# A second buffer for VectorE's first product, and four-column tiles moved by two transfers each, in a fused FFT filter and gated feed-forward kernel

## The chip, the cores and the metric

The kernel runs on one core of a Trainium2 chip. Its time is device time in microseconds, from launch to end, for one execution. The core has these engines: PE (TensorE, matrix products), DVE (VectorE), ACT (ScalarE), POOL (GpSimd) and SP (SyncE, which here issues every transfer). Sixteen DMA engines move the data between HBM and the on-chip memory SBUF. PE writes its products to a third memory, PSUM, from which VectorE and ScalarE read.

## The reference

The input x has 8 batches of 3136 rows and 256 columns. The reference filters each batch along its rows in the frequency domain and puts the result through a gated feed-forward layer:

```
X = rfft(x, axis=1)
y = irfft(X * (filt_r + 1j * filt_i), n=3136, axis=1)
h = relu(y @ w_in)                       # 256 -> 1024
c[s] = cw[0]*h[s-1] + cw[1]*h[s] + cw[2]*h[s+1]    # per column of h, zero at both ends
out = (h * sigmoid(c)) @ w_out           # 1024 -> 256
```

Everything is float32 for the filter. The weights of the second part come as float64 and are converted on the chip (`to_f32`, L154 to L174).

## The kernel before, in words

**Two parts.** The first part computes the filtered y as matrix products: 3136 = 28 x 112, so a transform of length 3136 is done as transforms of 112 and 28 with tables. It has four product stages, named `first` (L323), `second` (L330), `third` (L354) and `last_stage` (L210). Between `second` and `third`, `filt` (L341) multiplies with the filter. Between `first` and `second` and between `third` and `last_stage` the data is turned round through HBM, in `a_dram` and `b_dram`. The second part (from L420) is the feed-forward layer for all eight batches, in 448 passes; while it runs on batch b - 1, the last stage of batch b is done in small pieces between its passes.

**Groups.** In the first part the unit of work is a group: four of the 28 columns of a batch, 112 partitions of 4 x 256 float32 values. So each partition's row is 4 KB, and a tile is 448 KB. A batch has NQ = 7 groups, all batches 56.

**One turn of the loop** (L371 on, index i, with m = i - 9) does this, in the order of the program. On SP: load x of group i + 3 (`load`, L300), load a of group m + 1, load a part of the filter tables t1, t2 and of the table i1 in the turns 4 to 10 (`load_tables`, L255). On VectorE and POOL: `filt` of group m - 1. On PE: `first` of group i. ScalarE copies its product to a tile sa, which SP stores to `a_dram` (`store`, L310). On PE: `third` of group m - 2; ScalarE copies it to sb, which SP stores to `b_dram`. On PE: `second` of group m. Then, from turn 11, two steps of the weight conversion (`convert_weights`, L282), which run on VectorE, POOL and ScalarE. From turn 60 on, the last stage of batch 0 is done in seven steps of four columns (`last_load`, `last_stage`, `last_out`, L411 to L417).

**filt** makes three VectorE products from PSUM: `u = pp * t1` (L347), then two halves of v (L348 and L349), and POOL adds them, `z = u + v` (L351). u has one buffer. v has two fixed ones, `turned[0]` and `turned[1]`, chosen by `q % 2`, where q is the group's number in its batch. z and pp have two buffers each.

**Buffers and transfers.** x has four buffers, a three, sa and sb two each. A tile of the filter tables is 64 partitions of 4 KB. Each of these tiles is moved by one transfer. On the side of HBM, rows of x, a, b and the tables are contiguous for 4 KB, and those of the store to `a_dram` for 1 KB. Loads for the last stage (br, L197) are rows of 1 KB; batch 0 uses tiles of four columns with two buffers, the other batches tiles of two columns with four.

**Order.** All transfers go through SP's queue in the order of the program; a transfer that has to wait holds those behind it. The order of PE, VectorE, ScalarE and POOL is also that of the program (`manual_schedule`); semaphores between them are set by the tile framework, which also makes a new use of a buffer wait for the last reader of the old one.

Of the kernel before, what the change touches and what calls it, by code (L numbers as in the profile page):

```python
# [9 lines left out]
F32 = mybir.dt.float32  # L10
# [9 lines left out]
G = 28  # L20
D = 256
# [103 lines left out]
def tile_fft_filter_gated_ffn(  # L125
# [16 lines left out]
    nc = tc.nc  # L142
# [39 lines left out]
    a_dram = [dram.tile([N2, 112, D], F32, name=f"a_dram{b}") for b in range(B)]  # L182
    b_dram = [dram.tile([N2, 112, D], F32, name=f"b_dram{b}") for b in range(B)]
# [11 lines left out]
    lasts = {}  # L195

    def last_load(b, c, n=2):  # L197
        br = lp.tile([112, n, D], F32, name=f"br{n}", bufs=4 if n == 2 else 2)
        nc.sync.dma_start(out=br, in_=b_dram[b][c:c + n].rearrange("n p d -> p n d"))
        lasts[b, c] = br  # L200

# [32 lines left out]
    with (  # L234
# [12 lines left out]
        t1_sb = fc.tile([120, G, D], F32, name="t1_sb")  # L247
        t2_sb = fc.tile([120, G, D], F32, name="t2_sb")
# [6 lines left out]
        def load_tables(c):  # L255

            sl = slice(4 * c, 4 * c + 4)
            nc.sync.dma_start(out=t1_sb[0:64, sl], in_=fr[:, sl])
            nc.sync.dma_start(out=t2_sb[56:120, sl], in_=fi[:, sl])
            nc.sync.dma_start(out=i1_sb[:, sl], in_=i1[:, sl])  # L260

        def copy_filter(c):
# [37 lines left out]
        def load(kind, b, q):  # L300
            if kind == "x":
                r = xp.tile([112, 4, D], F32, name="x", bufs=4)
                v = x[b].rearrange("(p n) d -> p n d", n=N2)
            else:
                r = fp.tile([112, 4, D], F32, name="a", bufs=3)
                v = a_dram[b].rearrange("n (r g) d -> (n r) g d", g=G)
            nc.sync.dma_start(out=r, in_=v[:, 4 * q:4 * q + 4])
            rows[kind, b, q] = r

        def store(kind, b, q, ps):  # L310
            st = (xp if kind == "sa" else fp).tile([112, 4, D], F32, name=kind, bufs=2)
            nc.scalar.activation(st, ps, AF.Copy)  # L312
            sl = slice(4 * q, 4 * q + 4)
            if kind == "sa":
                v = a_dram[b][sl].rearrange("n p d -> p n d")
            else:
                v = b_dram[b].rearrange("n (r g) d -> (n r) g d", g=G)[:, sl]
            nc.sync.dma_start(out=v, in_=st)

        def bank_pair():  # L320
            return fps.tile([128, 1024], F32, name="ps")
# [19 lines left out]
        def filt(b, q):  # L341


            pp, v = psums.pop((b, q)), turned[q % 2]
            sl = slice(4 * q, 4 * q + 4)
            u = fp.tile([120, 4, D], F32, name="u", bufs=1)
            nc.vector.tensor_mul(u, pp, t1_sb[:, sl])  # L347
            nc.vector.tensor_mul(v[64:120], pp[0:56], t2_sb[0:56, sl])  # L348
            nc.vector.scalar_tensor_tensor(out=v[0:56], in0=pp[64:120], scalar=-1.0, in1=t2_sb[64:120, sl], op0=ALU.mult, op1=ALU.mult)  # L349
            z = fp.tile([120, 4, D], F32, name="z")  # L350
            nc.gpsimd.tensor_tensor(out=z, in0=u, in1=v, op=ALU.add)  # L351
            parts[b, q] = z
# [11 lines left out]
        for c in range(4):  # L364
            nc.sync.dma_start(out=s1_sb[:, 4 * c:4 * c + 4], in_=s1[:, 4 * c:4 * c + 4])
            load("x", 0, c)
# [3 lines left out]
        with tc.manual_schedule(engines=COMPUTE):  # L370
            for i in range(NI):  # L371
                m = i - SKEW
                if i == done:
# [4 lines left out]
                    lp = ctx.enter_context(tc.tile_pool(name="lp", bufs=2, side="right", reuse_waits="tile"))  # L378
                if i < 3:
                    nc.sync.dma_start(out=s1_sb[:, 4 * i + 16:4 * i + 20], in_=s1[:, 4 * i + 16:4 * i + 20])  # L380
                if (bp := at(i + 3)) and i:
                    load("x", *bp)
                if bp := at(m + 1):
                    load("a", *bp)
# [4 lines left out]
                if 4 <= i < 11:  # L389
                    load_tables(i - 4)  # L390
                if bp := at(m - 1):
                    filt(*bp)
                pf = first(*bp) if (bp := at(i)) else None
                if pf is not None:
                    store("sa", *at(i), pf)
                pt = third(*bp) if (bp := at(m - 2)) else None
                if pt is not None:
                    store("sb", *at(m - 2), pt)
# [12 lines left out]
                c = 4 * (i - done - 2)  # L411
# [4 lines left out]
                if 0 <= c < N2:  # L416
                    last_load(0, c, 4)  # L417
# [87 lines left out]
    with tc.manual_schedule(engines=COMPUTE):  # L505
        for m in range(NH + PLAG):
            if m + 4 in pieces:
                last_load(*pieces[m + 4])
            if a := at(m):
                inner(*a)  # L510
            if m in pieces:
                last_stage(*pieces[m], ps_h.tile([128, 512], F32, name="ps_h"))
            if a := at(m - PLAG):
                project(*a)
            if a := at(m - 1):
                relu(*a)
                conv(*a)
            if a := at(m - 2):
                gate(*a)
            if a := at(m - 3):  # L520
                split_g(*a)
            if m in pieces:
                last_out(*pieces[m])
            if a := at(m - PLAG):
                evacuate(*a)
# [44 lines left out]
```

## Time and profile before

| what | value |
|---|---|
| time, median of 3 runs | 1641.97 us (1640.53 to 1642.74) |
| profiled execution, its own time | 1637.69 us |
| its span, first to last instruction | 1635.6 us |
| PE busy | 1514.3 us, 93% |
| VectorE busy | 1301.1 us, 80% |
| ScalarE busy | 1171.9 us, 72% |
| POOL busy | 684.2 us, 42% |
| bytes moved | 166.74 MB in 105757 packets |
| granted TensorE clock, mean | 0.983 |

The profile is of one execution. Times in it are in microseconds from the span's start. L347 is line 347 of the kernel. A row of a timeline has the start, the length, the engine, the line, the operation, the tile written and the tiles read, the shapes, and in brackets the idle time before it with what ended it. "SPq" marks SP's issue of a transfer: its length is the issue, not the move. The DMA share is the time of the packets in flight, divided by sixteen engines and the length of the stretch; it can pass 1.00, because packets of one engine overlap a little. A shorter span of an engine that sits idle costs nothing, so what counts is the stage and what ends its waits.

### The profile page before, as it was taken

To read this page: it belongs to the slowest core of one execution; us is meant where nothing else is said; L and a number is where in the kernel's file an instruction comes from. 1 tells how busy PE (TensorE), PEld (TensorE's weight loads), DVE (VectorE), ACT (ScalarE), POOL (GpSimd) and SP (SyncE) were. 2 spreads that over 40 slices of the span, in tenths; PEclk is the share of its full clock that TensorE was granted. 3 is DMA by queue.
4 is the path that set the end of the run, shared out by engine and by line. 5 is a ranking of instruction groups with operands and counts; after the bars stand their busy time and mean duration, and the time that the engine had idled before them with its cause. 6 is when DMAs were issued, how large, how long until landed. Compare 5 with 4: busy or idle time off the path is not lost.

```text
span 1635.6 us, 25256 instructions
## 1 busy us (share of the span) xinstructions
PE 1514.3 (93%) x9424; PEld 1349.6 (83%) x9424; DVE 1301.1 (80%) x1790; ACT 1171.9 (72%) x2043; POOL 684.2 (42%) x568
## 2 busy tenths in 40 slices
PE   5587888887699999999999999999999999999999
PEld 4255555554589999999999999999999999999998
DVE  0388788855688888888888888888888888888887
ACT  2443333331488888888888888888888888888887
POOL 0144544443234444444444444444444444444444
PEclk8699999998999999999999999999999999999999
DMA  9999999986401101111111111111111111100001
GB/s 279 287 310 288 287 289 298 281 252 194 123 23 51 47 29 46 50 48 46 46 47 40 40 46 46 47 36 38 46 35 46 51 47 51 46 23 23 23 24 46
DMA packets 105757, 166.74 MB, mean 102 GB/s; under 512 B 6986, under 2 KB 83875, under 8 KB 105635
## 3 DMA queue, kind: packets, MB, share of 16 engines
q1 hardware_dynamic: 105635, 165.12, 33.7%
q8 instruction: 75, 1.23, 0.3%
q14 instruction: 47, 0.39, 0.1%
HBM read 88.03 MB, written 77.07 MB: 101 GB/s over the span
## 4 chain that ended last, share of the span: by engine, by line
PE 71%; DVE 1%; ACT 1%; issue 0%
PE ps_h L178 11%; PE ps_h L179 11%; PE ps_h L177 11%; PE po L476 11%; PE po L478 11%; PE po L477 11%; PE ps_h L219 5%; ACT y L146 1%; DVE y L149 1%; DVE t L451 0%; PE ps L219 0%; DVE t L450 0%; DVE t L456 0%; ACT sb L312 0%; ACT t L445 0%
## 5 line engine op out<-in xcount | busy, mean ns | idle before, releaser
L152 POOL TENSOR_TENSOR g<-t,g 128x448 fp32r<-128x448 f32 x448 | 517.2, 1155 | 677.9 <-ACT g L146 273.8
L476 PE MATMUL po<-wo,g 128*128 128x256 f32 x1568 | 441.5, 282 | 0.0
L478 PE MATMUL po<-wo,g 128*128 128x256 f32 x1568 | 433.7, 277 | 0.0
L477 PE MATMUL po<-wo,g 128*128 128x256 f32 x1568 | 433.4, 276 | 0.0
L450 DVE SCALAR_TENSOR_TENSOR t<-ps_h,cw,t 128x448 f32<-128x448 f32 x448 | 305.9, 683 | 82.1 <-ACT t L445 71.4
L178 PE MATMUL ps_h<-y,wi 128*128 128x450 f32 x896 | 330.4, 369 | 5.2 <-DVE y L149 5.2
L177 PE MATMUL ps_h<-y,wi 128*128 128x450 f32 x896 | 328.5, 367 | 3.6 <-ACT y L146 1.9
L179 PE MATMUL ps_h<-y,wi 128*128 128x450 f32 x896 | 328.7, 367 | 0.0
L451 DVE SCALAR_TENSOR_TENSOR t<-ps_h,cw,t 128x448 f32<-128x448 f32 x448 | 306.5, 684 | 16.0
L445 ACT ACTIVATE t<-ps_h,cw 128x448 f32<-128x448 f32 x448 | 285.2, 637 | 41.8 <-ACT ps_h L443 0.8
L476 PEld LDWEIGHTS po<-wo,g 128*128 128x128 f32 x1568 | 294.7, 188 | 7.0
L477 PEld LDWEIGHTS po<-wo,g 128*128 128x128 f32 x1568 | 294.3, 188 | 5.7
L478 PEld LDWEIGHTS po<-wo,g 128*128 128x128 f32 x1568 | 294.4, 188 | 0.0
L456 DVE TENSOR_TENSOR t<-ps_h,t 128x448 f32<-128x448 f32 x448 | 275.4, 615 | 0.1
L443 ACT ACTIVATE ps_h<-ps_h 128x450 f32<-128x450 f32 x448 | 251.5, 561 | 32.6 <-PE ps_h L179 28.0
L455 ACT ACTIVATE t<-t 128x448 f32<-128x448 f32 x448 | 254.9, 569 | 12.0 <-DVE t L451 10.8
L146 ACT ACTIVATE g<-t 128x448 fp32r<-128x448 f32 x448 | 254.4, 568 | 0.2 <-DVE t L456 0.2
L351 POOL TENSOR_TENSOR z<-u,v 120x1024 f32<-120x1024 f32 x56 | 142.7, 2548 | 249.7 <-DVE v L349 187.5
L178 PEld LDWEIGHTS ps_h<-y,wi 128*128 128x128 f32 x896 | 168.3, 188 | 14.3 <-DVE y L149 7.5
L177 PEld LDWEIGHTS ps_h<-y,wi 128*128 128x128 f32 x896 | 170.0, 190 | 11.9 <-ACT y L146 2.9
L179 PEld LDWEIGHTS ps_h<-y,wi 128*128 128x128 f32 x896 | 168.3, 188 | 13.9
L358 PE MATMUL ps<-z,i_sb 120*112 120x256 f32 x448 | 115.2, 402 | 68.1 <-POOL z L351 62.5
(51 smaller groups left out, 1411.3 us busy)
## 6 DMA issues: line engine op xcount, KB each, us to landing
x<-in_x SPq DMA_DIRECT2D x56, 448.0 KB, 6.1
a_dram<-sa SPq DMA_DIRECT2D x56, 448.0 KB, 5.3
a<-a_dram SPq DMA_DIRECT2D x56, 448.0 KB, 6.5
b_dram<-sb SPq DMA_DIRECT2D x56, 448.0 KB, 3.3
out<-ot SPq DMA_DIRECT2D x27, 896.0 KB, 4.1
br<-b_dram SPq DMA_DIRECT2D x98, 224.0 KB, 2.6
br<-b_dram SPq DMA_DIRECT2D x7, 448.0 KB, 4.7
raw<-in_w_in SPq DMA_DIRECT2D x8, 256.0 KB, 4.5
```

The lines of the kernel that those rows point to most:

```text
L146: nc.scalar.activation(dst, src, AF.Copy)
L152: nc.gpsimd.tensor_tensor(out=dst, in0=src, in1=hi.bitcast(F32), op=ALU.subtract)
L177: nc.tensor.matmul(ps, lhsT=wh, rhs=rh, start=start, stop=False, **kw)
L178: nc.tensor.matmul(ps, lhsT=wh, rhs=rl, start=False, stop=False, **kw)
L179: nc.tensor.matmul(ps, lhsT=wl, rhs=rh, start=False, stop=stop, **kw)
L445: nc.scalar.activation(t, h[:, 1:SUB + 1], AF.Copy, scale=cw[:, 1, f:f + 1])
L450: nc.vector.scalar_tensor_tensor(out=t, in0=h[:, 0:SUB], scalar=cw[:, 0, f:f + 1], in1=t, op0=ALU.mult, op1=ALU.add)
L451: nc.vector.scalar_tensor_tensor(out=t, in0=h[:, 2:SUB + 2], scalar=cw[:, 2, f:f + 1], in1=t, op0=ALU.mult, op1=ALU.add)
L456: nc.vector.tensor_mul(t, h[:, 1:SUB + 1], t)
L476: nc.tensor.matmul(o, lhsT=gh[:, sl], rhs=wo[0][:, f], start=first, stop=False, skip_group_check=True)
L477: nc.tensor.matmul(o, lhsT=gh[:, sl], rhs=wo[1][:, f], start=False, stop=False, skip_group_check=True)
L478: nc.tensor.matmul(o, lhsT=gl[:, sl], rhs=wo[0][:, f], start=False, stop=last, skip_group_check=True)
```

## The change

u gets the pool's usual two buffers. The transfers of x, a, sa, sb and of the filter tables t1 and t2 are each split into two, of two columns (2 KB a partition) each; for the store to `a_dram` the rows in HBM stay at 1 KB. The tile itself, and what waits for it, is as before: a product that reads a tile waits for both its halves. i1, the transform tables and the weights are moved as before. The tiles br of both sizes become one set of three buffers of four columns, of which a load of two columns uses the first half.

```diff
     def last_load(b, c, n=2):
-        br = lp.tile([112, n, D], F32, name=f"br{n}", bufs=4 if n == 2 else 2)
+        br = lp.tile([112, 4, D], F32, name="br", bufs=3)[:, 0:n]
...
             sl = slice(4 * c, 4 * c + 4)
-            nc.sync.dma_start(out=t1_sb[0:64, sl], in_=fr[:, sl])
-            nc.sync.dma_start(out=t2_sb[56:120, sl], in_=fi[:, sl])
+            for e in (4 * c, 4 * c + 2):
+                nc.sync.dma_start(out=t1_sb[0:64, e:e + 2], in_=fr[:, e:e + 2])
+                nc.sync.dma_start(out=t2_sb[56:120, e:e + 2], in_=fi[:, e:e + 2])
...
-            nc.sync.dma_start(out=r, in_=v[:, 4 * q:4 * q + 4])
+            for e in (0, 2):
+                nc.sync.dma_start(out=r[:, e:e + 2], in_=v[:, 4 * q + e:4 * q + e + 2])
             rows[kind, b, q] = r
...
-            sl = slice(4 * q, 4 * q + 4)
-            if kind == "sa":
-                v = a_dram[b][sl].rearrange("n p d -> p n d")
-            else:
-                v = b_dram[b].rearrange("n (r g) d -> (n r) g d", g=G)[:, sl]
-            nc.sync.dma_start(out=v, in_=st)
+            for e in (0, 2):
+                sl = slice(4 * q + e, 4 * q + e + 2)
+                if kind == "sa":
+                    v = a_dram[b][sl].rearrange("n p d -> p n d")
+                else:
+                    v = b_dram[b].rearrange("n (r g) d -> (n r) g d", g=G)[:, sl]
+                nc.sync.dma_start(out=v, in_=st[:, e:e + 2])
...
-            u = fp.tile([120, 4, D], F32, name="u", bufs=1)
+            u = fp.tile([120, 4, D], F32, name="u")
             nc.vector.tensor_mul(u, pp, t1_sb[:, sl])
```

## The prediction

> **What bounds the kernel now.** I read the page's head for the span, then the windows of busy time, to find the stage that the edit reaches.
>
> ```profile
> span 1635.6 us, 25256 instructions
> ```
>
> ```profile
> 20.00:69.78 49.78, 24.28 (x58) 14.00 (x59) 3.67 (x4) 15.61 (x15) 2.54 (x2) 0.62 1.05 283
> 69.78:97.16 27.38, 22.93 (x88) 14.91 (x86) 24.61 (x20) 15.56 (x15) 10.92 (x5) 1.00 1.02 322
> 69.78:331.51 261.73, 212.88 (x798) 138.64 (x796) 220.14 (x174) 91.63 (x99) 120.97 (x61) 1.00 0.96 292
> 331.51:400.92 69.41, 54.23 (x178) 33.44 (x179) 40.36 (x34) 17.00 (x18) 28.33 (x14) 0.93 0.74 219
> 440.00:1635.60 1195.60, 1181.15 (x8203) 1132.74 (x8201) 1010.43 (x1555) 1028.14 (x1895) 518.19 (x476) 1.00 0.13 41
> ```
>
> The columns of the second fence are the stretch, its length, then busy time and instructions of PE, PEld, DVE, ACT and POOL, the granted clock, the DMA share and GB/s. From 440 us on PE is busy 1181 of 1196 us and DMA 0.13: the edit's transfers and product aren't there. Everything it touches, but for the loads into br, lies in the first 440 us. I chose the ends of the middle stretches at starts of VectorE's first product u, which the view of one tile gives:
>
> ```profile
> L347 DVE TENSOR_TENSOR u<-pp,t_sb x40: 1223/1225/1227, 69.8 to 331.5; 120x1024 f32<-120x1024 f32 x40
> L347 DVE TENSOR_TENSOR u<-pp,t_sb x12: 1224/1225/1226, 331.5 to 400.9; 120x1024 f32<-120x1024 f32 x12
> ```
>
> So a turn of the loop (one group of four columns) takes 261.73/39 = 6.71 us, then 69.41/11 = 6.31 us. What sets it shows in the timeline.
>
> ```profile
> 183.99 1.23 DVE L347 TENSOR_TENSOR u<-pp,t_sb 120x1024 f32<-120x1024 f32 x1
> 185.22 1.22 DVE L348 TENSOR_TENSOR v<-pp,t_sb 56x1024 f32<-56x1024 f32 x1
> 186.46 1.23 DVE L349 SCALAR_TENSOR_TENSOR v<-pp,t_sb 56x1024 f32<-56x1024 f32 x1
> 187.71 0.69 DVE L168 SCALAR_TENSOR_TENSOR ws<-em 128x512 f32<-128x512 int32 x1
> 187.85 2.75 POOL L351 TENSOR_TENSOR z<-u,v 120x1024 f32<-120x1024 f32 x1 [4.18 <-DVE v L349]
> 188.44 2.45 DVE L170 TENSOR_SCALAR em<-ws 128x512 int32<-128x512 int32 x1
> 190.92 1.23 DVE L347 TENSOR_TENSOR u<-pp,t_sb 120x1024 f32<-120x1024 f32 x1
> ...
> 201.46 2.35 POOL L351 TENSOR_TENSOR z<-u,v 120x1024 f32<-120x1024 f32 x1 [2.69 <-PE pp L335]
> 203.84 1.22 DVE L347 TENSOR_TENSOR u<-pp,t_sb 120x1024 f32<-120x1024 f32 x1 [2.55 <-POOL z L351]
> ```
>
> With one u buffer the next u can't start before POOL has read the last one: u, v, v, z, u in a ring. At 203.84 u starts 0.03 us after z ended. In the turn from 183.99 to 190.92 the wait is covered: the weight conversion (L168, L170) fills VectorE until 190.89. Conversion steps come in a cycle of five turns, two of these heavy. VectorE's unavoidable work is 220.14/39 = 5.64 us a turn, PE's 212.88/39 = 5.46. The ring costs the difference to 6.71. But the DMA share in the same stretch is 0.96. So removing the ring exposes the DMA engines almost at once, and the forecast turns on what they can do.
>
> **The change, part by part.** Removed: the wait of u for the last z. Left of the ring are v's two fixed buffers, picked by q % 2. With seven groups in a batch, q = 6 and the next q = 0 share one, so once in seven turns v still waits for z: v, v, z is 1.22 + 1.23 + 2.75 and some 0.3 of releases, 5.5 us, under the forecast turn. That costs nothing here.
>
> Term A, 69.78 to 331.51 us. With the ring gone a turn has three bounds. VectorE has 5.64 us of work in the mean. The two heavy turns of five stay at 6.94 us if nothing smooths them. A third turn holds the conversion step L162:
>
> ```profile
> L162 DVE TENSOR_SCALAR em<-raw 128x512 int32<-128x512 int32 x7 | 15.9, 2265 | 0.0
> ```
>
> That is 3.7 us of products, 2.27, and an estimated 0.4 for the short step ahead of it, 6.4 us; the two light turns fall to PE's 5.5. The five sum to 31.3, so 6.26 a turn. PE: 5.46. The ring z, third, second, product over two turns is below. DMA: a turn moves 292 GB/s x 6.71 us = 1.96 MB at share 0.96. If the price per byte stays and the share rises to 1.00, 1.02 or 1.05 (the last was held from 20 to 69.78 us), a turn is 6.44, 6.32 or 6.13 us; at the 322 GB/s of the first 27 us of this stretch it is 6.09. I take 6.25: among the DMA figures, and the unsmoothed VectorE's figure. Bounds 6.1 and 6.5. That is 39 x (6.71 - 6.25) = 17.9 us less, bounds 24 and 8.
>
> Does a 2 KB row have the price of a 4 KB one? No view tells the 2 KB packets apart, so I bound it by stretches with other mixes.
>
> ```profile
> q1 hardware_dynamic: 46272, 45.42, 13.0%
> ...
> q1 hardware_dynamic: 31453, 67.55, 95.1%
> ...
> DMA packets 803, 2.14 MB, mean 267 GB/s; under 512 B 94, under 2 KB 426, under 8 KB 803
> q1 hardware_dynamic: 803, 2.14, 101.9%
> ```
>
> These are packets, MB and share of 16 engines. The first is 460 to 1600 us, where all is rows of 1 KB: 0.130 x 16 x 1140 us / 45.42 MB = 52 ns per KB. The second is 97.16 to 331.51 us, mostly rows of 4 KB by bytes: 0.951 x 16 x 234.35 / 67.55 = 53 ns. The third is 3 to 11 us, rows of 4 KB and 1.75 KB in one direction: 61 ns. Rows of 1 KB and of 4 KB cost the same here; what moves the price is the direction or the crowding. 2 KB lies between them, so I price the split at nothing per byte, with 3% either way (0.2 us a turn), inside the bounds above. The Trainium skill speaks against this edit: its page Perfetto Trace Analysis, section DMA Optimizations, calls batching small rows, from 2 KB to 4 KB or 8 KB, a dramatic gain in throughput. By that rule the split would raise the turn; the 52 and 53 ns don't bear it out, and how far it could go is the first rival.
>
> The issues double. SyncE's queue in one turn:
>
> ```profile
> 179.90 0.30 SPq L318 DMA_DIRECT2D b_dram<-sb  x1
> 180.30 0.48 SPq L307 DMA_DIRECT2D x<-in_x  x1
> 180.83 0.77 SPq L307 DMA_DIRECT2D a<-a_dram  x1
> 183.35 0.32 SPq L318 DMA_DIRECT2D a_dram<-sa  x1
> ```
>
> Four issues take 1.87 us; eight take up to 3.7 of 6.25, so the queue keeps up. It is in order: a half that waits holds everything behind it, the store after a load too. A second limit shows in its waits and landings:
>
> ```profile
> SPq L260 <- DMA x<-in_x: 3.9, 4, 1.4
> ...
> x<-in_x SPq DMA_DIRECT2D x39, 448.0 KB, 5.9
> a<-a_dram SPq DMA_DIRECT2D x39, 448.0 KB, 6.6
> ```
>
> A load of i1 (L260) waits for a landing of x, with which it shares no data. In those turns x, two table parts, i1 and sa are issued, so that x lies eight issues back: a landing counter seems to come round every eighth transfer. Whole transfers take two turns to come round; halves take one. So each half must land within one turn. The slowest, a, lands after 6.6 us as a whole; less bytes stand ahead of a half (0.23 MB less at 292 GB/s is 0.8 us), 5.8 us, under 6.25. I price it at nothing and keep 6.6 us a turn as a rival.
>
> Term B, 331.51 to 400.92 us, eleven turns. The loads of x end here and DMA falls to 0.74. For the first five turns first() still runs, and PE's 5.46 us is the bound. After that the ring over two turns counts:
>
> ```profile
> 381.47 1.23 DVE L347 TENSOR_TENSOR u<-pp,t_sb 120x1024 f32<-120x1024 f32 x1 [2.54 <-POOL z L351]
> 385.35 2.34 POOL L351 TENSOR_TENSOR z<-u,v 120x1024 f32<-120x1024 f32 x1 [3.92 <-PE pp L335]
> 387.74 1.98 PE L358 MATMUL ps<-z,i_sb 120*112 120x256 f32 x8 [2.56 <-POOL z L351]
> 389.56 1.88 PE L335 MATMUL pp<-a,s_sb 112*120 112x512 f32 x4
> ```
>
> From u to the end of second() behind third() is 391.44 - 381.47 = 9.97 us; that second() feeds the product two turns on, so 5.0 us a turn, 5.1 with releases. 5 x 5.46 + 6 x 5.1 = 57.9 instead of 69.4: 11.5 us less, bounds 13 and 6 (PE's clock, 0.93 here, may fall further).
>
> Behind 400.92 another chain holds:
>
> ```profile
> 427.56 1.95 PE L358 MATMUL ps<-z,i_sb 120*112 120x256 f32 x8 [1.33 <-DVE y L149]
> ```
>
> third() waits for the last stage's output on VectorE, not for z, and I give these turns nothing.
>
> Term C, the start. Up to 69.78 us DMA is the bound (share 1.05), with the price per byte unchanged. The first x is complete one issue later, about 0.4 us, and a few more issues stand ahead of the first store. I take 1.5 us more, bounds 3 less (halves free the window earlier) and 5 more.
>
> Term D, br. Three shared buffers stand in place of four small and two large.
>
> ```profile
> SPq L199 <- PE ps_h L219: 682.3, 94, 27.2
> br<-b_dram SPq DMA_DIRECT2D x98, 224.0 KB, 2.6
> ```
>
> SyncE stands at L199 until a buffer comes free; then the load takes 2.6 us. With three it waits for the stage three pieces back, not four; out's stores are queued behind it, and they wait for later work anyhow. Pieces lie some three to four passes apart, a pass 1195.6/448 = 2.7 us, so the load still lands two pieces, over 16 us, ahead. Price nothing; without that cover 2.6 us for each late load.
>
> Sum: 17.9 + 11.5 - 1.5 = 27.9 us less. The profiled execution took 1637.69 us (span 1635.6), so 1609.8; the median of the three runs is 4.3 above it, so 1614.1.
>
> **The rivals.** *Rows of 2 KB cost more (slower).* With the ring gone, DMA is the bound from 0 to 331.51 us, so a rise f of its price costs f x (70 + 39 x 6.25) = f x 314 us against 27.9 gained: it decides at f = 9%. At 15% the time is 1642 + 19 = 1661 us. Against it stand 52 and 53 ns; for it, that no view separates the packets of 2 KB. 6%. It is the way in which the rule of the Trainium skill's page Perfetto Trace Analysis, section DMA Optimizations, would act here.
>
> *The DMA engines are full already, or the window of eight holds the turn at a's 6.6 us.* Then A gives 39 x 0.11 = 4, B 9 and C -1: 1630 us. For it: share 0.96, and 283 GB/s at 1.05 early on. Against it: 322 GB/s from 69.78 to 97.16 us, with more than one direction in flight, and halves land sooner. 18%.
>
> *DMA has room.* Its share counts packets in flight and may fall when they overlap better; then VectorE's 5.64 is the turn, A gives 42, and the time is 1642 - 52 = 1590 us; that asks 1.96 MB in 5.64 us, 348 GB/s, above the 322 of the best stretch here. 11%.
>
> *The wait stays* by v's pair or by another release in the ring: 1642 us. The code shows one pair per parity, so 2%.
>
> **How the numbers follow.** The forecast has 63%, its own range 1604 to 1631 by the bounds of the terms. The range 1601 to 1634 takes in the full-DMA rival and leaves out the first and third. A measurement of this kernel can tell about 0.2%, 3.3 us, from no change. Faster by more: the forecast, the third rival and most of the second, 0.88. Within: the last one and the second's edge, 0.05. Slower: the first rival and mishaps of the window, 0.07.
>
> **What would show it.** Right: u no longer waits for z; a turn near 6.25 up to about 312 us, DMA share 1.0 or above, PE or VectorE waiting for a; then turns near 5.1 to 5.5; the stretch behind unchanged in length, begun some 28 us sooner. Wrong: DMA below 0.95 with turns under 5.9; or more than 58 ns per KB; or SyncE waiting long at its loads for landings; or waits for br behind 440 us.

## The result

| kernel | median us | runs | ratio to before, 95% interval |
|---|---|---|---|
| before | 1641.25 | 4 | |
| changed | 1601.09 (1598.09 to 1602.87) | 4 | 0.9755 [0.9734, 0.9776] |

The changed kernel is 40 us faster by the medians, where 27.9 were forecast. The range of 1601 to 1634 holds it, at the very edge. The profiled execution took 1602.23 us against 1637.69, 35.5 us less, and its parts can be set beside the terms of the forecast.

The first view is the windows of busy time of the changed kernel, cut at the same events as before: the second u, the u 39 turns on, and the u eleven turns after that. The columns are as in the prediction.

```profile
20.00:67.52 47.52, 21.63 (x57) 12.13 (x57) 3.67 (x4) 15.61 (x15) 2.58 (x2) 0.70 1.04 286
67.52:308.98 241.46, 210.04 (x796) 140.24 (x796) 220.23 (x174) 90.62 (x98) 119.06 (x60) 1.00 0.99 316
308.98:366.14 57.16, 48.77 (x180) 31.18 (x178) 40.36 (x34) 18.02 (x19) 29.51 (x15) 1.00 0.82 254
405.10:1600.50 1195.40, 1181.85 (x8192) 1133.22 (x8192) 1009.31 (x1555) 1027.58 (x1894) 518.50 (x476) 1.00 0.13 41
```

The view of u's tile gives the same ends:

```profile
L350 DVE TENSOR_TENSOR u<-pp,t_sb x40: 1223/1225/1226, 67.5 to 309.0; 120x1024 f32<-120x1024 f32 x40
...
L350 DVE TENSOR_TENSOR u<-pp,t_sb x12: 1223/1225/1225, 309.0 to 366.1; 120x1024 f32<-120x1024 f32 x12
```

The 39 turns of term A take 241.46/39 = 6.19 us each instead of 6.71, 20.3 us less. The eleven of term B take 57.16 instead of 69.41, 12.2 us less. The start is over at 67.52 instead of 69.78, 2.3 us less. These sum to 34.8 of the span's 35.1 us. The last stretch, with the loads of br, is as long as before to about 1 us. Its starts, at 405.10 and 440, are not one event; from the same step of y on (404.54 here and 440.82 before) it takes 1196.0 against 1194.8.

The timeline shows what a turn is made of now (rows of VectorE, and z on POOL):

```profile
172.31 2.45 DVE L166 TENSOR_SCALAR em<-raw 128x512 int32<-128x512 int32 x1
...
177.27 1.23 DVE L352 SCALAR_TENSOR_TENSOR v<-pp,t_sb 56x1024 f32<-56x1024 f32 x1
178.52 0.69 DVE L168 SCALAR_TENSOR_TENSOR ws<-em 128x512 f32<-128x512 int32 x1
178.66 2.75 POOL L354 TENSOR_TENSOR z<-u,v 120x1024 f32<-120x1024 f32 x1 [4.18 <-DVE v L352]
179.25 2.45 DVE L170 TENSOR_SCALAR em<-ws 128x512 int32<-128x512 int32 x1
...
181.73 1.23 DVE L350 TENSOR_TENSOR u<-pp,t_sb 120x1024 f32<-120x1024 f32 x1
```

The second u buffer is there, and still this u starts 0.32 us after z ended (178.66 + 2.75 = 181.41). What stands between them is the conversion step L170. It ends at 181.70, 0.29 us after z. In the turns without such a step u no longer waits for z. Five turns in a row took 6.67, 6.94, 6.94, 6.65 and 6.25 us before; they take 6.71, 6.97, 6.94, 4.47 and 6.04 now, so the gain comes almost all from the two light ones, the fourth above all. The view of waits on VectorE had one row of u and z in this stretch before:

```profile
DVE u L347 <- POOL z L351: 37.9, 16, 2.6
```

It has none any more:

```profile
DVE u L350 <- PE pp L338: 13.5, 7, 2.4
DVE u L350 <- issue: 8.4, 1, 8.4
DVE u L350 <- ACT wo L146: 2.4, 1, 2.4
DVE v L351 <- POOL z L354: 1.0, 1, 1.0
```

So the open questions were three: which part of the edit gives what; whether the DMA engines, now at a share of 0.99, hold the turn at 6.19; and whether L162, L166 and L170 are long work or a hidden wait for z.

### The profile page after: what moved, and what is told of

Read it like the earlier page. It is cut to its first block, busy times and chain, and to the rows that moved or that the text cites. A ratio compares the mean times of both kernels' runs of the same rounds, so it can differ in the third digit from the quotient of the medians.

```text
span 1600.5 us, 25622 instructions
## 1 busy us (share of the span) xinstructions
PE 1503.6 (94%) x9424; PEld 1347.4 (84%) x9424; DVE 1300.6 (81%) x1790; ACT 1172.4 (73%) x2043; POOL 684.9 (43%) x568
## 4 chain that ended last, share of the span: by engine, by line
PE 73%; DVE 1%; ACT 1%; issue 0%
PE ps_h L178 12%; PE ps_h L179 11%; PE ps_h L177 11%; PE po L479 11%; PE po L481 11%; PE po L480 11%; PE ps_h L219 5%; ACT y L146 1%; DVE y L149 1%; PE ps L219 0%; DVE t L454 0%; DVE t L453 0%; DVE t L459 0%; ACT sb L314 0%; ACT t L448 0%
## 5 line engine op out<-in xcount | busy, mean ns | idle before, releaser
L149 DVE TENSOR_TENSOR y<-ps_h,y 128x448 fp32r<-128x448 f32 x98 | 103.2, 1053 | 77.3 <-ACT y L146 77.3
```

## The experiments

Ratios are to the runs of the kernel before on the same chip; their medians were 1638.5 to 1638.9 us. "Second u" is its start, and "turn" is term A's stretch divided by 39, both from the one profiled execution.

| kernel | median us | ratio, 95% interval | second u | turn |
|---|---|---|---|---|
| u and br alone (e1_u_br) | 1603.27 | 0.9791 [0.9774, 0.9809] | 69.49 | 6.19 |
| split alone (e2_split_only) | 1632.16 | 0.9958 [0.9942, 0.9975] | 65.25 | 6.71 |
| changed, masks for shifts (e4_cheap) | 1599.17 | 0.9761 [0.9742, 0.978] | 65.69 | 6.19 |
| u and br, masks (e6_cheap_whole) | 1606.74 | 0.9806 [0.9787, 0.9826] | 68.42 | 6.19 |
| changed, steps moved (e7_moved) | 1579.18 | 0.963 [0.9611, 0.9649] | 65.09 | 5.69 |
| u and br, steps moved (e8_moved_whole) | 1581.26 | 0.9655 [0.9632, 0.9678] | 69.02 | 5.65 |
| tiles shared by partitions (e9_by_partitions) | 1642.81 | 1.0024 [1.0009, 1.0038] | 73.36 | 6.71 |
| split, one u, steps moved (e10_moved_u1) | 1645.88 | 1.0048 [1.0033, 1.0063] | 63.94 | 7.06 |
| loads split alone (f1_loads) | 1632.09 | 0.9964 [0.9951, 0.9977] | 64.49 | 6.71 |
| stores split alone (f2_stores) | 1637.75 | 0.9997 [0.9987, 1.0006] | 67.80 | 6.71 |
| quarters (f3_quarters) | 1723.92 | 1.0518 [1.0503, 1.0532] | 89.18 | 8.28 |

**The second buffer and the split, each alone.** The buffer can't be had without the change to br: with the old br tiles the pool of 16 KB a partition doesn't fit beside a second u, 13.06 KB are left. So the two go together.

```diff
-            u = fp.tile([120, 4, D], F32, name="u", bufs=1)
+            u = fp.tile([120, 4, D], F32, name="u")
...
-        br = lp.tile([112, n, D], F32, name=f"br{n}", bufs=4 if n == 2 else 2)
+        br = lp.tile([112, 4, D], F32, name="br", bufs=3)[:, 0:n]
```

> The second u buffer and the shared br tiles alone; every tile is moved whole, as before. First theory (VectorE's turns with long conversion steps, and the ring of z, third, second and the product over two turns, set the 6.19 us a turn; the split rows do little): a turn of 6.2 to 6.3 us, about 1603 us, and the start stays at 67.5 to 70 us. Second theory (the DMA engines set the turn, as forecast, and rows of 2 KB are cheaper, 50 against 52.5 ns per KB): whole rows bring the turn to 6.4 to 6.5, 1609 to 1613 us. Third theory (the split does most of the work): 1625 us or more.

The other kernel has the split of the loads, stores and tables, and u and br as before.

> The split transfers alone, with one u buffer and the old br tiles. First theory: u waits for z as before, a turn stays at 6.7 us, about 1639 us, with at most 2 us won at the start. Second theory: the same, since the ring hides the transfers: 1636 to 1641 us. Third theory: 1620 us or less.

With whole transfers the turn is 6.19 us too, to the hundredth. The view of u's tile, for the buffer alone and then for the split alone:

```profile
L347 DVE TENSOR_TENSOR u<-pp,t_sb x40: 1223/1224/1225, 69.5 to 310.9; 120x1024 f32<-120x1024 f32 x40
```

```profile
L350 DVE TENSOR_TENSOR u<-pp,t_sb x40: 1223/1225/1225, 65.3 to 326.9; 120x1024 f32<-120x1024 f32 x40
```

The second theory, mine, wanted 6.4 to 6.5 us of the whole transfers. It falls: the DMA engines don't set the turn. The third falls too. The buffer gives 35 of the 40 us. The split alone gives 6.3 us by the medians. In its profiled execution the second u comes 4.5 us earlier, and the turns are as before. That is more than the first two theories had put on record, and far less than the third.

**Work or wait: shorter conversion steps.** L162, L166 and L170 each do two shifts. One masking gives the same values.

```diff
-        v.tensor_scalar(m, high, 30, 30, op0=ALU.logical_shift_right, op1=ALU.logical_shift_left)
+        v.tensor_scalar(m, high, 0, -0x40000000, op0=ALU.logical_shift_left, op1=ALU.bitwise_and)
...
-        v.tensor_scalar(m, high, 27, 0xF, op0=ALU.logical_shift_right, op1=ALU.bitwise_and)
+        v.tensor_scalar(m, high, 0, 0x78000000, op0=ALU.logical_shift_left, op1=ALU.bitwise_and)
...
-        v.tensor_scalar(e, dst.bitcast(I32), 23, 23, op0=ALU.logical_shift_right, op1=ALU.logical_shift_left)
+        v.tensor_scalar(e, dst.bitcast(I32), 0, -0x800000, op0=ALU.logical_shift_left, op1=ALU.bitwise_and)
```

(The comparison behind the second one has 7 x 2^27 for 7.)

> The changed kernel with the three long conversion steps (two shifts each, 2.3 to 2.5 us) written as one masking each, the same values from steps as short as L160's 0.43 us. VectorE's work falls by some 6 us per five turns, to about 4.5 us a turn. First theory: the heavy turns vanish, and a turn falls to the ring's 5.3 to PE's 5.5 us: 39 x 0.7 = 27 us, about 1575 us. Second theory: the DMA engines already hold 316 GB/s at a share of 0.99 and keep the turn at 6.0 to 6.2 us: 1594 to 1601 us.

> Second u buffer and shared br tiles, whole transfers, and the short conversion steps: the comparison of split with whole where VectorE isn't in the way. First theory (split rows do little): within 4 us of the run with short steps and split rows. Second theory (the DMA engines bind, and whole rows cost 5% more per byte): the turn is 0.3 us longer than with split rows, 12 us more, and some 2 us more at the start.

With split transfers the time did not move, and by the expectation's own words that would speak for the second theory. It doesn't, since the premise failed: the steps are no shorter. The groups of VectorE from 90 to 307 us, with masks:

```profile
L166 DVE TENSOR_SCALAR em<-raw 128x512 int32<-128x512 int32 x7 | 17.2, 2455 | 0.2
L170 DVE TENSOR_SCALAR em<-ws 128x512 int32<-128x512 int32 x7 | 17.2, 2452 | 0.2
...
L160 DVE TENSOR_SCALAR em<-raw 128x512 int32<-128x512 int32 x7 | 3.0, 427 | 0.2
```

Another operation takes the same 2.45 us, and L160, one shift and one mask on the same shape, takes 0.43. So the operation is not what takes the time. What differs is the place: L160 starts before z of its turn, the others while z runs. The kernel with whole transfers and masks fits neither of its two theories: its turn is the same 6.19 us, but it is 7.6 us slower by the medians than the one with split transfers, where at most 4 or some 14 us were expected.

**Work or wait: the steps elsewhere.** From there came a new theory: a step of this kind that starts while POOL works on z stands still until z ends. To try it, the two steps of a turn are issued between the two v products. By then the z of the group before has ended, and the z of this group can't start yet.

```diff
-        def filt(b, q):
+        def filt(b, q, steps):
...
             nc.vector.tensor_mul(v[64:120], pp[0:56], t2_sb[0:56, sl])
+            for _ in range(steps):
+                next(wsteps, None)
...
-                    filt(*bp)
+                    filt(*bp, 2 if i >= 11 else 0)
...
-                    if i >= 11:
-                        next(wsteps, None)
```

> The changed kernel with the two conversion steps of a turn issued between the two v products instead of behind them, so that POOL's z of the group before has ended when they come. First theory (port): the 2.45 us of L162, L166 and L170 are waits for z, and the steps themselves take some 0.3 us each; placed there they don't wait, the turns of 6.94 us vanish, and the turn falls from 6.19 to between PE's 5.5 and the 5.9 that the DMA engines allow: 12 to 27 us less than the changed kernel, 1574 to 1589 us. Rival (work): the steps take 2.3 to 2.5 us of VectorE wherever they stand, and delay z as well: the turn stays at 6.2 or grows, 1601 us or more.

> The same move with whole transfers (second u buffer, shared br tiles). If the DMA engines are the next bound and rows of 2 KB are cheaper (50 against 52.5 ns per KB), the turn is 0.3 us longer than with split transfers, 12 us, and the start 2 to 3 us later. If PE or the ring is the next bound, only the start differs: 2 to 6 us more than with split transfers.

> The move of the conversion steps with split transfers but one u buffer. First theory (port): the steps no longer wait for z, but now stand inside the ring u, v, steps, v, z, and lengthen it from 6.24 by their own 0.7 us in the mean to 6.9: 5 to 8 us more than the split transfers alone, 1637 to 1641 us. Rival (work): with 2.45 us steps inside the ring a turn grows to about 8 us, 1680 us.

The timeline of VectorE in the changed kernel with the steps moved, and the group rows of u and of the same steps:

```profile
158.05 1.22 DVE L351 TENSOR_TENSOR v<-pp,t_sb 56x1024 f32<-56x1024 f32 x1
159.30 0.69 DVE L164 TENSOR_TENSOR em<-em 128x512 int32<-128x512 int32 x1
160.03 0.43 DVE L166 TENSOR_SCALAR em<-raw 128x512 int32<-128x512 int32 x1
160.48 1.23 DVE L354 SCALAR_TENSOR_TENSOR v<-pp,t_sb 56x1024 f32<-56x1024 f32 x1
162.50 1.23 DVE L350 TENSOR_TENSOR u<-pp,t_sb 120x1024 f32<-120x1024 f32 x1 [0.79 <-PE pp L338]
```

```profile
L350 DVE TENSOR_TENSOR u<-pp,t_sb 120x1024 f32<-120x1024 f32 x39 | 47.8, 1225 | 49.4 <-PE pp L338 31.7 <-issue 6.7 <-PE pp L341 5.1
...
L162 DVE TENSOR_SCALAR em<-raw 128x512 int32<-128x512 int32 x8 | 3.4, 430 | 0.0
L166 DVE TENSOR_SCALAR em<-raw 128x512 int32<-128x512 int32 x8 | 3.4, 427 | 0.3
L170 DVE TENSOR_SCALAR em<-ws 128x512 int32<-128x512 int32 x8 | 3.4, 427 | 0.3
```

The same instruction with the same shift constants takes 0.43 us instead of 2.45. The wait is gone, and the turn falls to 5.69. The theory of the work falls. z is shorter too, as the view of its tile shows, for the changed kernel and then with the steps moved (nanoseconds, least, median and most):

```profile
L354 POOL TENSOR_TENSOR z<-u,v x39: 2349/2754/2769, 71.3 to 308.4; 120x1024 f32<-120x1024 f32 x39
```

```profile
L356 POOL TENSOR_TENSOR z<-u,v x39: 2342/2353/2365, 69.7 to 286.1; 120x1024 f32<-120x1024 f32 x39
```

That a long step is a wait for z is shown by these runs; what holds it is not in the trace. The Trainium skill's page SBUF — State Buffer, section Who interferes with whom, has a cause that fits: VectorE and GpSimd share a pair of SBUF ports under an exclusive lock. A tensor_scalar in a two-port mode takes it, an operation with two SBUF inputs contends for its read side, and whoever comes second stands still for the whole of the other's instruction. The trace agrees, in both directions: L170 comes behind z and ends 0.29 us after it; and z, issued 0.14 us behind L168 (0.69 us, two SBUF inputs), takes 2.75 us instead of 2.35, 0.40 more, where L168 had 0.55 left. No view names the mode in which a tensor_scalar runs.

With the wait gone, what is the next bound? The windows of the two kernels with moved steps, first with split and then with whole transfers:

```profile
65.09:287.15 222.06, 211.40 (x792) 137.93 (x792) 172.73 (x173) 91.62 (x100) 110.21 (x61) 1.00 1.05 342
```

```profile
69.02:289.39 220.37, 209.74 (x792) 137.62 (x792) 172.75 (x174) 91.74 (x100) 110.27 (x61) 1.00 1.04 342
```

PE is busy 95% of both, and u's longest wait is for pp from PE: PE is the next bound, or close to it. The DMA engines move 342 GB/s with split and with whole transfers, where I had taken 322 as the most. VectorE's busy time has fallen from 220 to 173 us: the 47 us between were waits counted as work. The expectation of a turn 0.3 us longer with whole rows failed: it is 0.04 shorter, and only the start differs, as the other branch had it. The kernel with the steps moved and the split kept has the lowest median of all, 1579.18 us, 0.963 [0.9611, 0.9649] of the kernel before; its interval overlaps that of the one with whole transfers.

With one u buffer the move does harm, as the first theory had it, but by more: the turn is 7.06 us where 6.9 was expected, since the four turns of five that hold steps grow by 0.3 to 0.5 us, the two heavy ones from 6.94 to 7.45. So the second buffer pays alone, 35 us, but moving the steps pays only with it: there the turn falls from 6.19 to 5.69, and with one buffer it rises from 6.71 to 7.06.

**What in the split helps the start.** Three kernels on the base of the one before.

> The kernel before with the loads alone (x, a, the two filter tables) split by columns. The split of loads and stores together won 0.42%, about 6 us, all of it ahead of the first groups of VectorE. If the loads' shorter rows are what is cheaper (57 against 59 ns per KB in the start, which is mostly loads): 4 to 6 us less than before, 1632 to 1635 us, and the second u starts at about 65 to 66 us. If the stores are: no change.

> The kernel before with the stores alone (sa, sb) split by columns. If the gain is the loads': within 2 us of before, the second u at 69 to 70 us. If halves of stores, which land sooner and free ScalarE's two sa buffers sooner, are the gain: 4 to 6 us less, the second u at 65 to 66 us.

The loads alone give the whole gain, the stores none that can be measured in the time, though the second u of the one profiled execution came 2 us earlier. The windows of the start, loads split and then stores split (they end about 1 us behind the second u):

```profile
20.00:65.40 45.40, 23.87 (x60) 13.69 (x59) 4.57 (x4) 15.60 (x15) 2.37 (x2) 0.70 1.06 298
```

```profile
20.00:69.00 49.00, 23.91 (x64) 14.02 (x65) 4.89 (x5) 15.61 (x15) 2.57 (x2) 0.69 1.05 287
```

At nearly the same share the engines move 298 GB/s against 287. One execution says little here: the changed kernel, which has the split loads too, moved 286. The second u is the surer sign. It starts at 63.94 to 67.52 us in the six kernels with the loads split in two by columns, and at 67.80 to 69.78 in the five with whole loads. To tell the shorter row from the larger number of transfers, the tiles were shared by partitions instead, with rows of 4 KB (the edit of the loads; tables and stores likewise):

```diff
-            nc.sync.dma_start(out=r, in_=v[:, 4 * q:4 * q + 4])
+            for h in (slice(0, 64), slice(64, 112)):
+                nc.sync.dma_start(out=r[h], in_=v[h, 4 * q:4 * q + 4])
```

> The kernel before with one u buffer and its old br tiles, each tile moved by two transfers that share it by partitions (64 and 48 of 112, 32 and 32 of 64), so that rows stay at 4 KB. The split by columns won about 6 us (0.42%). If the shorter row won it, nothing here: 1636 to 1642 us. If more and shorter transfers in the queue won it, the same 6 us: 1630 to 1634 us.

This wins nothing; the second u even comes 3.6 us later than before. So twice as many transfers of half the bytes do not help by themselves. That it is the row is likely, not shown: a half by partitions also spreads over the DMA engines in another way. What would happen with yet shorter rows can't be read from the quarters, which hit another limit first:

> The kernel before with all these tiles moved by four transfers of one column each, rows of 1 KB. If the start's price falls with the row (59 ns per KB at 4 KB, 57 at 2 KB), it falls again or stays: 1630 to 1634 us. If the window of eight outstanding transfers, now two tiles, or SyncE's issues (16 in a turn of 6.7 us, some 0.4 us each) bind: slower than before, a turn of 7 us or more, 1650 us or more.

Its timeline of SyncE's queue:

```profile
200.34 1.80 SPq L309 DMA_DIRECT2D x<-in_x  x4
202.19 1.83 SPq L309 DMA_DIRECT2D a<-a_dram  x4
204.13 1.94 SPq L321 DMA_DIRECT2D a_dram<-sa  x4
206.19 1.89 SPq L321 DMA_DIRECT2D b_dram<-sb  x4
208.18 1.80 SPq L309 DMA_DIRECT2D x<-in_x  x4
```

Sixteen issues fill 7.84 us (200.34 to 208.18) with hardly a gap. By this SyncE is the bound, as the second branch allowed; the DMA share in the stretch from 100 to 300 us falls to 0.80, and a turn takes 8.28 us. The window of eight isn't what binds: these quarters land after 2.2 to 2.7 us.

## Why the prediction was right, and where it was not

*The sum.* In the profiled executions 34.8 us were gained where 27.9 were forecast: 2.4 more in term A, 0.7 in B and 3.8 in C. The other 5 of the 40 us are mostly the scatter of single executions: the profiled one of the kernel before lay 3.6 us under its median, that of the changed kernel 1.1 us over. That the median fell 0.09 us inside the range is luck.

*The ring of u.* Right: the buffer alone gives 35 us, and in the turns without long steps u no longer waits for z.

*Term A.* The size held, 20.3 us against 17.9, a turn of 6.19 against 6.25. Its reasons held in half. The sum of VectorE's unsmoothed turns (31.3 over five, two of them at 6.94) is what the trace has: 6.71, 6.97, 6.94, 4.47 and 6.04 us, 31.1 in all. Singly only the two heavy ones fit: the turn with L162 was put at 6.4, and the light ones at 5.5 each. The figures of the DMA engines, which the text called the thing on which the forecast turns, had no part in it: whole and split transfers give the same turn, and 342 GB/s went through later. That they gave nearly the same turn was luck. Two of the signs named for them did not come: the share was 0.99, not 1.0 or above, and PE's waits for a come to under 3 us in the whole stretch. The failed step is "if the price per byte stays": the price is time in flight, and it went from 52.5 ns per KB before to 50 in the changed kernel and 49 with the steps moved (1.046 x 16 x 222.06 us / 75.75 MB):

```profile
DMA packets 51063, 75.93 MB, mean 342 GB/s; under 512 B 5285, under 2 KB 22946, under 8 KB 51048
...
q1 hardware_dynamic: 51048, 75.75, 104.6%
```

A share near 1.00 did not mean that the engines were full.

*"VectorE's unavoidable work is 5.64 us a turn."* Wrong: it is 172.73/39 = 4.43. The rest was z's wait inside busy instructions. The quoted timeline had it: L170 ended at 190.89, z at 190.60.

*The price of the split rows.* In term A nothing, as forecast. With the steps moved the price was 49.1 ns per KB with split and 48.5 with whole transfers; as PE was busy 95% of both, this says that neither width held the turn up, not which could carry more. In the start the split of the loads was a gain. The Trainium skill's page Perfetto Trace Analysis, section DMA Optimizations, says that batching small transfers, such as 2 KB into 4 or 8 KB, can improve throughput dramatically. It speaks of transfers, and to read it as a rule for rows was the prediction's step; no run here shows such a loss at rows of 2 KB.

*Term B.* 12.2 us against 11.5: the turns are 5.20 us in the mean. Up to 341 us PE is busy 30.27 of 32.02 us, and behind that it waits for z, as forecast. The steps moved leave the turns at 5.12.

*Term C, the start.* Wrong in sign: 2.3 us less instead of 1.5 more, and 4.5 less with the split alone. The step that failed is the price per byte, taken as unchanged: worked as in term A, it went from 59 ns per KB before to 58 in the changed kernel and 57 with the split alone. The split of the loads is what helps; why it does stays open, the shorter row being likely.

*Term D, br.* Nothing, as forecast.

*Rivals.* The dearer row and the full DMA engines are refuted by the runs. "DMA has room" was true of the DMA engines; its price wasn't, because VectorE's blocked steps held the turn until they were moved. "The wait stays" held in three turns of five, where u still starts only after z: VectorE's long step, which stands before u, waits for z without a release in the code.

## What to carry to other kernels

When a buffer is doubled, look for a second wait under the first: an instruction of VectorE that always ends just after one of GpSimd's, and is several times shorter elsewhere, is waiting and not working, however busy it looks. Place such steps where GpSimd is idle. And a DMA share near one is not yet a bound; the same traffic with another order of work tells.

## What the runs showed of the hardware that was not expected

- A VectorE tensor_scalar on 128x512 int32 takes 0.43 us clear of GpSimd and 2.45 us when issued behind its sum of 120x1024 floats, and the profile counts all of it as busy.
- Sixteen DMA engines carried 342 GB/s over 220 us, in a mix of loads and stores with rows of 1 to 4 KB, while the start of the kernel before, mostly loads, held 283 at the same share of 1.05.
- SyncE issues one transfer each 0.49 us (7.84 us for sixteen) when it does nothing else.
